# The first MoE's transposes, logits and block ends at a distance of four units instead of three

## The chip, the cores and the metric

The kernel runs on one core of a Trainium2 chip. The metric is the time of one execution on the device in microseconds (us), taken as the median of several runs. TensorE is called PE here (PEld is its weight load), VectorE DVE, ScalarE ACT, GpSimd POOL; SP only issues transfers.

## What is computed

Three layers in a row, all in float32: a clustered attention, a dense MoE with a rational activation, and a soft MoE. The change is in the middle one, with x the attention's output (1536 tokens by 512) and W_in 512 by 2048:

```
h = x @ w_in
P = a[0] + a[1]*h + a[2]*h**2 + a[3]*h**3
Q = 1.0 + abs(b[0])*abs(h) + abs(b[1])*h**2
g = P / (Q + 1e-6)
x2 = g @ w_out
logits = x2 @ phi                  # start of the soft MoE
d = softmax(logits over the tokens);  slot_input = d.T @ x2
c = softmax(logits over the slots);   out = c @ experts(slot_input)
```

The kernel never forms x2: it multiplies w_out by phi beforehand (`wphi`), so that the logits are g @ wphi, and it gathers d.T @ g before it multiplies by w_out.

## The kernel before

**The work.** The first MoE has three blocks of 512 tokens (`NB`), and each block sixteen units of 128 hidden columns (`NF`), so 48 units (`nunit`). A unit goes through five steps, each a small function:

- `h_mm(n)`: twelve matmuls on PE (lines L809, L810, L812) give the product h of unit n, 128 by 512, in one of three PSUM banks (`psH`). Two tiles of w_in (`w_load`, L652) have to be there.
- `s1(n)`: ACT makes u = |h| (L838) and the first linear term p (L839); POOL makes q from u (L840, L842); DVE goes on with p (L841, L843). L843 is the last to read h.
- `s2(n)`: ACT takes the reciprocal of q as exp(-ln q) into r, in one of two PSUM banks (L849, L850).
- `s3(n)`: DVE forms g with three operations (L857, L858, L859). L859 reads two SBUF tiles, q and p, and its result is g, held in the tile p.
- `s4(n)`: PE transposes g (four transposes, L870) into one of two PSUM banks, and ACT copies it to a buffer (L871). At every fourth unit PE also adds the logits of the last four units (eight matmuls, L876), and only then their four tiles p come free. At the sixteenth, DVE copies the logits out (L880).

After a block's sixteenth unit, `block_end` gives five steps, of which one is taken in each of the following turns: e0 (`lsum`, L892; DVE L893), e0b (transposes `lt`, L902, and ACT's exponentials, L905), e2 (transposes `dt`, L926), e3 (`dg`, 32 matmuls, L934, the gathering of g) and e1.

**The order.** The loop over n writes the order of PE and SP by hand: in turn n PE does `h_mm(n)`, then `s4(n - 3)`, then one step of a block end if there is one. PE's queue runs in this order, so whatever waits in `s4(n - 3)` holds `h_mm(n + 1)`. The order on ACT, DVE and POOL is made by the framework's planner, which plays the program through with costs of its own and takes instructions as they become ready there. On the chip each engine's queue runs strictly in that order. After the last product the loop runs three more turns, in which `warm(k)` puts 3, 4 and 1 matmuls on PE whose results nobody reads.

**After the loop** the last block end, the multiplication by w_out and the experts follow, fed by 1 MB weight loads (`wt`, L789) into buffers as these come free.

Of the kernel before, what the change touches and what calls it, by code (L numbers as in the profile page):

```python
# [8 lines left out]
F32 = mybir.dt.float32  # L9
# [53 lines left out]
def tile_kernel(ctx, tc, qT, kT, v, cenT, cenP, consts, constsb, ab, w_in, w_out, phi, w1, w2, out, dbg=None):  # L63
# [10 lines left out]
    NF = DFF // 128  # L74
# [574 lines left out]
    def w_load(n):  # L649
        for a in range(2):  # L650
            wsp[n, a] = w_p.tile([128, NCC, 128], F32R, tag="w", name="w")
            SP.dma_start(wsp[n, a].rearrange("p c n -> p (c n)").bitcast(F32),  # L652
                         w_in2[n % NF][:, a].rearrange("p c n -> p (c n)"))
# [38 lines left out]
    for n in range(-LEAD, NSL + 1):  # L692
        p, k = divmod(n, 12)
# [62 lines left out]
    g_p = bctx.enter_context(tc.tile_pool(name="gp", bufs=2, reuse_waits="tile"))  # L756
# [7 lines left out]
    def sl_tile(dt, name):  # L764
        return sl_p.tile([128, 4, 512], dt, tag="sl", name=name)
# [18 lines left out]
    def freed(alloc, n=1):  # L784
        for _ in range(n):
            if queue:
                key, src = queue.pop(0)
                t = alloc(F32, "wt").rearrange("p a b -> p (a b)")
                SP.dma_start(t, src)  # L789
                W[key] = (t, alloc)  # L790
# [8 lines left out]
    nunit = NB * NF  # L799
# [17 lines left out]
    def parts(n):  # L817

        return (slice(0, 256), slice(256, 512)) if n == nunit - 1 else (slice(0, 512),)

    def s1(n):

        h = hp.pop(n)
        u = g_p.tile([128, 512], F32, tag="u", name="u")
        q = g_p.tile([128, 512], F32, tag="q", name="q", bufs=4)
        p = g_p.tile([128, 512], F32, tag="g", name="p", bufs=7)
        sp[n] = dict(q=q, p=p)
        if n == nunit - 1:
            for w in parts(n):
                ACT.activation(u[:, w], h[:, w], AF.Abs)  # L830
                POOL.tensor_scalar(q[:, w], u[:, w], b_1, b_0, ALU.mult, ALU.add)
                POOL.tensor_tensor(q[:, w], q[:, w], u[:, w], ALU.mult)
            for w in parts(n):
                ACT.activation(p[:, w], h[:, w], AF.Identity, bias=a_n[2], scale=a_n[3])
                DVE.tensor_tensor(p[:, w], p[:, w], h[:, w], ALU.mult)
                DVE.scalar_tensor_tensor(p[:, w], p[:, w], a_n[1], h[:, w], ALU.add, ALU.mult)
            return
        ACT.activation(u, h, AF.Abs)  # L838
        ACT.activation(p, h, AF.Identity, bias=a_n[2], scale=a_n[3])  # L839
        POOL.tensor_scalar(q, u, b_1, b_0, ALU.mult, ALU.add)  # L840
        DVE.tensor_tensor(p, p, h, ALU.mult)  # L841
        POOL.tensor_tensor(q, q, u, ALU.mult)  # L842
        DVE.scalar_tensor_tensor(p, p, a_n[1], h, ALU.add, ALU.mult)  # L843
# [18 lines left out]
    def s4(n):  # L862
        t, f = divmod(n, NF)
        j, k = divmod(f, 4)
        g = gts[n]
        if k == 0:
            gsl[t, j] = sl_tile(F32, f"g{t}{j}")
        ps = psT.tile([128, 512], F32, tag="t", name="gt")
        for i in range(4):
            PE.transpose(ps[:, i * 128:(i + 1) * 128], g[:, i * 128:(i + 1) * 128], ident)  # L870
        ACT.copy(gsl[t, j][:, :, k * 128:(k + 1) * 128], ps.rearrange("p (i f) -> p i f", i=4))  # L871
        if k == 3:
            if j == 0:
                lps[t] = psL.tile([128, 512], F32, tag="l", name="l")
            for kk in range(4):
                PE.matmul(lps[t][32 * kk:32 * kk + 32, :], wphi[:, 4 * j + kk, :], gts.pop(n - 3 + kk),  # L876
                          start=(j == 0), stop=(j == 3))
            if j == 3:
                Ls[t] = keep.tile([128, 512], F32, tag="L", name="L")
                DVE.tensor_copy(Ls[t], lps.pop(t))  # L880


    def block_end(t):

        hold = {}
        nM, nM0 = mxs[:, t % 2:t % 2 + 1], mxs[:, 1 - t % 2:2 - t % 2]
        Sm, corr, sb = (mxs[:, i:i + 1] for i in range(2, 5))

        def e0():
            ps = psT.tile([128, 512], F32, tag="t", name="lsum")  # L890
            dT = hold["dT"] = Ls.pop(t)
            PE.matmul(ps, sum4, dT, start=True, stop=True)  # L892
            DVE.tensor_scalar(dT, ps, -1.0, None, ALU.mult, ALU.min, accum_out=nM)  # L893
            if t:
                DVE.tensor_tensor(nM, nM, nM0, ALU.min)

        def e0b():
            dT = hold["dT"]

            lt = psT.tile([128, 512], F32, tag="t", name="lt")  # L900
            for i in range(4):
                PE.transpose(lt[:, i * 128:(i + 1) * 128], dT[:, i * 128:(i + 1) * 128], ident)  # L902
            if t == NB - 1:
                hold["dT"] = a_tile("dT")
            ACT.activation(hold["dT"], dT, AF.Exp, scale=-1.0, bias=nM, accum_out=sb if t else Sm)  # L905
            if t:
                ACT.activation(corr, nM0, AF.Exp, scale=-1.0, bias=nM)
                DVE.scalar_tensor_tensor(Sm, Sm, corr, sb, ALU.mult, ALU.add)
            lv = lt.rearrange("p (i r s) -> p i r s", i=4, r=4)[:, :, 0, :]
            cm = keep.tile([128, 4], F32, tag="cm", name="cm")  # L910
            DVE.tensor_reduce(cm, lv, AX.X, ALU.min)
            DVE.tensor_tensor(ce[t], cm.unsqueeze(2).to_broadcast([128, 4, 32]), lv, ALU.subtract)

        def e1():
            cs = keep.tile([128, 4], F32, tag="cs", name="cs")
            c = ce[t]
            ACT.activation(c, c, AF.Exp)
            DVE.tensor_reduce(cs, c, AX.X, ALU.add)
            DVE.tensor_scalar(cs, cs, 1e-9, None, ALU.add)
            DVE.reciprocal(cs, cs)  # L920
            DVE.tensor_tensor(c, c, cs.unsqueeze(2).to_broadcast([128, 4, 32]), ALU.mult)

        def e2():
            ps = psT.tile([128, 512], F32, tag="t", name="dt")
            for i in range(4):
                PE.transpose(ps[:, i * 128:(i + 1) * 128], hold["dT"][:, i * 128:(i + 1) * 128], ident)  # L926
            d = hold["d"] = hold["dT"].rearrange("p (i s) -> p i s", i=4)
            ACT.copy(d, ps.rearrange("p (i s) -> p i s", i=4))

        def e3():  # L930
            ps = psT.tile([128, 512], F32, tag="t", name="dg")
            for i in range(4):
                for j in range(4):
                    PE.matmul(ps[32 * j:32 * j + 32, :], hold["d"][:, i, 32 * j:32 * j + 32], gsl[t, j][:, i, :],  # L934
                              start=(i == 0), stop=(i == 3))
            if t == 0:
                DVE.tensor_copy(U, ps)
            else:
                DVE.scalar_tensor_tensor(U, U, corr, ps, ALU.mult, ALU.add)
            if t == NB - 2:  # L940
                waiting.append(sl_tile)
            if t == NB - 1:
                freed(sl_tile, 4)

        return [e0, e0b, e2, e3, e1]

    def warm(k):

        for _ in range(k):
            ps = psH.tile([128, 512], F32, tag="h", name="warm")  # L950
            PE.matmul(ps[:, 0:256], ident, cst[:, 0:256], start=True, stop=True)

    ends = []


    manual = tc.manual_schedule(engines={mybir.EngineType.PE, mybir.EngineType.SP})
    manual.__enter__()
    for n in range(nunit + 3):
        if n + WAHEAD < nunit:
            w_load(n + WAHEAD)  # L960
        if waiting and n >= 3 and n % 3 == 0:
            freed(waiting.pop(0))
        if n < nunit:
            h_mm(n)
        if 0 <= n - 3:
            s4(n - 3)
            if (n - 3) % NF == NF - 1:
                ends += block_end((n - 3) // NF)
        if ends and (n - 3) % NF != NF - 1:
            ends.pop(0)()  # L970
        if n < nunit:
            s1(n)
        if 0 <= n - 1 < nunit:
            s2(n - 1)
        if n >= nunit:
            warm((3, 4, 1)[n - nunit])
        if 0 <= n - 2 < nunit:
            s3(n - 2)
    manual.__exit__(None, None, None)
# [12 lines left out]
    def a_tile(name, dt=F32):  # L992
        return a_p.tile([128, 512], dt, tag="a", name=name)
# [197 lines left out]
```

## Time and profile before

| what | value |
|---|---|
| median of 3 runs | 597.94 us (597.42 to 599.94) |
| the profiled execution, its own time | 601.37 us |
| its span, first to last instruction | 599.6 us |
| mean granted clock of TensorE | 0.989 of full |
| first MoE, first product to last transposes and logits | 337.3 to about 535 us |
| PE and DVE busy over the span | 557.7 us (93%) and 468.7 us (78%) |

The profiled execution is 3.43 us above the median; its span is 1.8 us shorter than its own time. Idle time is given in front of the instruction that ended it, with the instruction that released it. A matmul's duration reaches beyond the start of the next, as they are pipelined; the step from one start to the next tells the cost.

### The profile page before, as it was taken

How to read it: one execution, taken by the hardware profiler on the slowest of the kernel's cores; microseconds unless marked ns; L12 is line 12 of the kernel's file. 1: busy time of each engine (PE TensorE's matmuls, PEld its weight loads, DVE VectorE, ACT ScalarE, POOL GpSimd, SP SyncE). 2: the span in 40 equal slices, each digit the busy share in tenths (PEclk: the TensorE clock that was granted, in tenths of full speed). 3: DMA queues.
4: the chain of work that ended last, by engine and by line, in shares of the span. 5: the costliest groups of instructions: out<-in, count | busy, mean ns of one | idle time of the engine just before them, and what ended most of it. 6: DMA issues, size and time to landing. Idle time of an engine off the chain costs nothing.

```text
span 599.6 us, 9906 instructions
## 1 busy us (share of the span) xinstructions
PE 557.7 (93%) x3343; PEld 344.6 (57%) x3346; DVE 468.7 (78%) x817; ACT 393.2 (66%) x713; POOL 377.4 (63%) x487
## 2 busy tenths in 40 slices
PE   8899999999989999999899989999999999978995
PEld 3465555565555655555555667776667757753363
DVE  5779788798787987988984299999899998962033
ACT  3667777787677776787686487777578767740111
POOL 8749899697996988979658365565366545611000
PEclk9989999999999999999999999999999999989999
DMA  8613563354424633244343366766477547379996
GB/s 225 230 37 116 163 192 138 110 181 159 168 89 165 200 117 123 75 137 150 125 157 125 126 224 227 266 210 215 154 270 231 197 164 276 94 293 366 420 419 257
DMA packets 37906, 113.77 MB, mean 190 GB/s; under 512 B 5216, under 2 KB 5664, under 8 KB 33248
## 3 DMA queue, kind: packets, MB, share of 16 engines
q1 hardware_dynamic: 37856, 113.14, 54.1%
q8 instruction: 26, 0.43, 0.3%
q14 instruction: 24, 0.20, 0.1%
HBM read 96.02 MB, written 15.73 MB: 186 GB/s over the span
## 4 chain that ended last, share of the span: by engine, by line
PE 47%; DVE 26%; ACT 10%; POOL 8%; issue 7%; DMA 1%; SPq 0%; DVEq 0%; POOLq 0%; ACTq 0%
DVE neg L393 5%; PE s L383 5%; PE av L472 4%; PE s L458 4%; PE h L809 3%; PE h L812 3%; PE h L810 3%; PE s L384 3%; DVE p L859 3%; PE s L459 3%; PE pb L1042 3%; PE pb L1113 2%; DVE mh L564 2%; ACT neg L401 2%; DVE p L858 2%
## 5 line engine op out<-in xcount | busy, mean ns | idle before, releaser
L393 DVE TENSOR_SCALAR_CACHE_REDUCE neg<-s 128x768 f32<-128x768 f32 x96 | 91.3, 951 | 38.3 <-ACT neg L401 26.1
L463 ACT ACTIVATE e<-s 128x768 f32<-128x768 f32 x96 | 77.5, 807 | 58.3 <-PE s L459 58.2
L401 ACT ACTIVATE neg<-neg,nv 128x768 f32<-128x768 f32 x96 | 89.4, 932 | 9.2 <-DVE neg L393 8.9
L383 PE MATMUL s<-k,q 128*128 128x384 f32 x192 | 76.5, 398 | 13.3 <-DVE neg L393 9.5
L840 POOL TENSOR_SCALAR q<-u,babs 128x512 f32<-128x512 f32 x47 | 40.3, 858 | 75.9 <-ACT u L838 75.9
L472 PE MATMUL av<-e,vt 128*64 128x384 f32 x384 | 83.2, 512 | 0.2 <-ACT e L463 0.2
L809 PE MATMUL h<-xh,w 128*128 128x512 f32 x192 | 80.7, 420 | 0.0
L383 PEld LDWEIGHTS s<-k,q 128*128 128x128 f32 x192 | 36.6, 191 | 68.3 <-DVE neg L393 26.8
L810 PE MATMUL h<-xl,w 128*128 128x512 f32 x192 | 75.9, 395 | 0.0
L458 PE MATMUL s<-q,k 128*128 128x384 f32 x192 | 73.1, 381 | 0.7 <-DVE neg L393 0.5
L842 POOL TENSOR_TENSOR q<-q,u 128x512 f32<-128x512 f32 x47 | 63.8, 1357 | 3.9
L384 PE MATMUL s<-k,q 80*128 80x384 f32 x192 | 65.5, 341 | 0.0
L459 PE MATMUL s<-q,k 128*128 128x384 f32 x192 | 64.7, 337 | 0.0
L812 PE MATMUL h<-xh,w 128*128 128x512 f32 x192 | 52.7, 396 | 0.0
L579 POOL TENSOR_TENSOR w<-mh,ex 128x512 f32<-128x512 f32 x32 | 44.3, 1383 | 10.6 <-DMA w_out<-w 5.3
L859 DVE SCALAR_TENSOR_TENSOR p<-q,p 128x512 f32<-128x512 f32 (+1 forms) x49 | 49.2, 1005 | 0.1
L849 ACT ACTIVATE r<-q,epsc 128x512 f32<-128x512 f32 (+1 forms) x49 | 33.5, 684 | 21.9 <-POOL q L842 20.6
L838 ACT ACTIVATE u<-h 128x512 f32<-128x512 f32 x47 | 27.8, 591 | 27.7 <-PE h L812 27.7
L809 PEld LDWEIGHTS h<-xh,w 128*128 128x128 f32 x192 | 36.2, 189 | 16.9 <-issue 10.3
L458 PEld LDWEIGHTS s<-q,k 128*128 128x128 f32 x192 | 36.0, 188 | 16.2 <-issue 8.3
L841 DVE TENSOR_TENSOR p<-p,h 128x512 f32<-128x512 f32 x47 | 31.8, 677 | 16.9 <-ACT p L839 16.8
L812 PEld LDWEIGHTS h<-xh,w 128*128 128x128 f32 x192 | 36.3, 189 | 8.9
(193 smaller groups left out, 1219.3 us busy)
## 6 DMA issues: line engine op xcount, KB each, us to landing
wt<-w SPq DMA_DIRECT2D x32, 1024.0 KB, 8.0
w<-w_in SPq DMA_DIRECT2D x96, 256.0 KB, 3.1
raw<-w_in SPq DMA_DIRECT2D x16, 512.0 KB, 3.6
raw<-w_out SPq DMA_DIRECT2D x16, 512.0 KB, 3.4
w_in<-w SPq DMA_DIRECT2D x16, 512.0 KB, 2.7
rawk<-kT SPq DMA_DIRECT2D x14, 384.0 KB, 4.0
rawq<-qT SPq DMA_DIRECT2D x14, 384.0 KB, 3.6
w_out<-w SPq DMA_DIRECT2D x16, 256.0 KB, 3.3
```

The lines of the kernel that those rows point to most:

```text
L383: PE.matmul(ps[:, c, 0:HS], o["q1"][:, it], o["k1"][:, w], start=True, stop=False)
L384: PE.matmul(ps[:, c, 0:HS], o["q2"][0:80, it], o["k2"][0:80, w], start=False, stop=True)
L393: DVE.tensor_scalar(neg, s1s.pop((p, idx))[:, :, 0:HS], -1.0, None, ALU.mult, ALU.min, accum_out=nvs[p, half][0][:, 0, col:col + 1])
L401: ACT.activation(neg, neg, AF.Exp, scale=-1.0, bias=nv[:, 0, col:col + 1], accum_out=ssum[:, col:col + 1])
L458: PE.matmul(ps[:, h, 0:HS], o["k1"][:, jt], o["q1"][:, w], start=True, stop=False)
L459: PE.matmul(ps[:, h, 0:HS], o["k2"][:, jt], o["q2"][:, w], start=False, stop=True)
L463: ACT.activation(e, s2s.pop((p, k))[:, :, 0:HS], AF.Exp)
L472: PE.matmul(a[64 * h:64 * h + 64, 0:HS], vs[p][:, h, j, :], e[:, h, :], start=(j == 0), stop=(j == 5))
L809: PE.matmul(h, wh[:, c, :], xh[t][:, c, :], start=(c == 0), stop=False)
L810: PE.matmul(h, wh[:, c, :], xl[t][:, c, :], start=False, stop=False)
L812: PE.matmul(h, wl[:, c, :], xh[t][:, c, :], start=False, stop=(c == NCC - 1))
L859: DVE.scalar_tensor_tensor(p[:, w], q[:, w], 2.0, p[:, w], ALU.subtract, ALU.mult)
```

## The change

The distance becomes a constant, `LAG = 4`. Transposes, logits and block ends of unit n - 4 now follow the product of unit n on PE. There is one more turn at the end, with one more warming matmul in its place in the list, and the tiles p have eight buffers in place of seven, since each now lives one turn longer.

```
-        p = g_p.tile([128, 512], F32, tag="g", name="p", bufs=7)
+        p = g_p.tile([128, 512], F32, tag="g", name="p", bufs=8)
...
+    LAG = 4
...
-    for n in range(nunit + 3):
+    for n in range(nunit + LAG):
         if n + WAHEAD < nunit:
             w_load(n + WAHEAD)
         if waiting and n >= 3 and n % 3 == 0:
             freed(waiting.pop(0))
         if n < nunit:
             h_mm(n)
-        if 0 <= n - 3:
-            s4(n - 3)
-            if (n - 3) % NF == NF - 1:
-                ends += block_end((n - 3) // NF)
-        if ends and (n - 3) % NF != NF - 1:
+        if 0 <= n - LAG:
+            s4(n - LAG)
+            if (n - LAG) % NF == NF - 1:
+                ends += block_end((n - LAG) // NF)
+        if ends and (n - LAG) % NF != NF - 1:
             ends.pop(0)()
         if n < nunit:
             s1(n)
         if 0 <= n - 1 < nunit:
             s2(n - 1)
         if n >= nunit:
-            warm((3, 4, 1)[n - nunit])
+            warm((1, 3, 4, 1)[n - nunit])
         if 0 <= n - 2 < nunit:
             s3(n - 2)
```

## Rows read from the trace of the kernel before

**Rows 1.** The page's first part: busy time of each engine, its share of the span, its instructions.

```profile
PE 557.7 (93%) x3343; PEld 344.6 (57%) x3346; DVE 468.7 (78%) x817; ACT 393.2 (66%) x713; POOL 377.4 (63%) x487
```

**Rows 2.** The first MoE cut into six stretches (view of stretches, core 0). Columns: from:to in us, length, then busy us (and instructions) of PE, PEld, DVE, ACT, POOL, then the granted TensorE clock, DMA share and GB/s.

```profile
345.00:411.00 66.00, 62.90 (x312) 46.48 (x311) 64.24 (x91) 51.78 (x91) 39.05 (x36) 1.00 0.69 237
411.00:437.00 26.00, 24.96 (x145) 17.80 (x145) 23.42 (x38) 16.75 (x31) 12.80 (x12) 1.00 0.51 177
437.00:476.00 39.00, 37.62 (x189) 27.18 (x188) 38.19 (x53) 30.95 (x54) 22.78 (x22) 1.00 0.68 235
476.00:503.00 27.00, 25.89 (x149) 18.63 (x148) 24.31 (x42) 17.86 (x34) 13.02 (x13) 1.00 0.55 193
503.00:525.00 22.00, 21.31 (x110) 15.36 (x108) 21.39 (x31) 17.60 (x32) 13.38 (x12) 1.00 0.45 149
525.00:535.00 10.00, 7.44 (x38) 5.33 (x36) 7.41 (x15) 5.19 (x12) 2.92 (x4) 0.83 0.75 310
```

**Rows 3.** The groups by line inside 337 to 525 us, one of POOL's and the five DVE operations of a unit. Columns: line, engine, operation, tiles, shapes, count | busy us, mean ns | idle us before them and what ended it.

```profile
L859 DVE SCALAR_TENSOR_TENSOR p<-q,p 128x512 f32<-128x512 f32 x45 | 46.5, 1034 | 0.1
...
L840 POOL TENSOR_SCALAR q<-u,babs 128x512 f32<-128x512 f32 x47 | 40.3, 858 | 75.9 <-ACT u L838 75.9
...
L843 DVE SCALAR_TENSOR_TENSOR p<-p,ncoef,h 128x512 f32<-128x512 f32 x47 | 34.7, 737 | 0.4
...
L857 DVE SCALAR_TENSOR_TENSOR q<-q,epsc,r 128x512 f32<-128x512 f32 x46 | 33.9, 737 | 1.2 <-ACT r L850 1.1
...
L858 DVE SCALAR_TENSOR_TENSOR p<-p,ncoef,r 128x512 f32<-128x512 f32 x46 | 33.9, 736 | 0.0
...
L841 DVE TENSOR_TENSOR p<-p,h 128x512 f32<-128x512 f32 x47 | 31.8, 677 | 16.9 <-ACT p L839 16.8
```

**Rows 4.** The waits between 330 and 540 us: who waited for whom, us in total, times, longest us.

```profile
DVE p L841 <- ACT p L839: 16.8, 9, 8.8
...
PE gt L870 <- DVE p L859: 7.7, 13, 2.6
```

**Rows 5.** DVE in order of time, the instructions before which it sat idle. Columns: start us, duration us, engine, line, operation, tiles, count, [idle us before it <- what ended it].

```profile
341.70 0.69 DVE L841 TENSOR_TENSOR p<-p,h 128x512 f32<-128x512 f32 x1 [8.77 <-ACT p L839]
...
344.51 0.69 DVE L841 TENSOR_TENSOR p<-p,h 128x512 f32<-128x512 f32 x1 [1.34 <-ACT p L839]
...
370.11 0.69 DVE L841 TENSOR_TENSOR p<-p,h 128x512 f32<-128x512 f32 x1 [0.73 <-ACT p L839]
...
435.50 0.69 DVE L841 TENSOR_TENSOR p<-p,h 128x512 f32<-128x512 f32 x1 [2.45 <-ACT p L839]
...
496.78 0.69 DVE L841 TENSOR_TENSOR p<-p,h 128x512 f32<-128x512 f32 x1 [0.60 <-ACT p L839]
...
500.27 0.69 DVE L841 TENSOR_TENSOR p<-p,h 128x512 f32<-128x512 f32 x1 [2.02 <-ACT p L839]
```

**Rows 6.** PE in order of time around the first block end (same columns).

```profile
418.94 0.63 PE L926 MATMUL dt<-cst,L 128*128 128x128 f32 x4 [1.04 <-ACT p L839]
419.32 0.48 PE L809 MATMUL h<-xh,w 128*128 128x512 f32 x1
...
422.74 1.07 PE L876 MATMUL l<-p,wphi 128*32 128x512 f32 x8
423.62 3.62 PE L934 MATMUL dg<-g,L 128*32 128x512 f32 x32
427.17 0.50 PE L809 MATMUL h<-xh,w 128*128 128x512 f32 x1
...
430.44 0.48 PE L809 MATMUL h<-xh,w 128*128 128x512 f32 x1
```

**Rows 7.** DVE and then POOL in order of time at 511 to 515 us (same columns).

```profile
512.04 1.50 DVE L859 SCALAR_TENSOR_TENSOR p<-q,p 128x512 f32<-128x512 f32 x1
513.47 0.67 DVE L841 TENSOR_TENSOR p<-p,h 128x512 f32<-128x512 f32 x1
514.07 0.68 DVE L859 SCALAR_TENSOR_TENSOR p<-q,p 128x512 f32<-128x512 f32 x1
...
511.70 1.30 POOL L842 TENSOR_TENSOR q<-q,u 128x512 f32<-128x512 f32 x1
514.09 1.31 POOL L840 TENSOR_SCALAR q<-u,babs 128x512 f32<-128x512 f32 x1 [1.09 <-ACT u L838]
```

**Rows 8.** DVE and then PE in order of time near 400 us: the last read of product 15 (L843), the first matmul of product 18 (L809).

```profile
399.03 0.73 DVE L843 SCALAR_TENSOR_TENSOR p<-p,ncoef,h 128x512 f32<-128x512 f32 x1
...
401.67 0.48 PE L809 MATMUL h<-xh,w 128*128 128x512 f32 x1
```

**Rows 9.** The tail of the first MoE: the last half of DVE's last unit, PE's transposes of units 45 and 47, and three stretches of 2 us (columns as in rows 2).

```profile
532.53 0.42 DVE L859 SCALAR_TENSOR_TENSOR p<-q,p 128x256 f32<-128x256 f32 x1
...
527.80 0.63 PE L870 MATMUL gt<-cst,p 128*128 128x128 f32 x4 [2.56 <-DVE p L859]
...
533.41 0.60 PE L870 MATMUL gt<-cst,p 128*128 128x128 f32 x4
...
528.00:530.00 2.00, 2.00 (x9) 1.67 (x8) 1.52 (x3) 1.74 (x5) 0.24 (x1) 0.65 1.01 422
530.00:532.00 2.00, 2.00 (x8) 1.67 (x7) 1.98 (x6) 0.45 (x2) 0.00 (x0) 0.50 1.03 434
532.00:534.00 2.00, 2.00 (x15) 1.60 (x18) 0.91 (x2) 0.16 (x1) 0.00 (x0) 0.99 0.47 197
```

## The prediction

> **What bounds the kernel now.** I read the page first: PE is busy for 93% of the span and DVE for 78% [rows 1]. Those are means over three layers, so I cut the first MoE into stretches [rows 2]. There DVE is as full as PE: 64.24 of 66 us between 345 and 411, 38.19 of 39 between 437 and 476, 21.39 of 22 between 503 and 525. Only the two stretches that hold a block end differ: 23.42 of 26 and 24.31 of 27, so DVE is idle for 2.6 and 2.7 us there.
>
> The groups by line say why DVE is full [rows 3]. A unit's five operations have means of 1034, 737, 737, 736 and 677 ns. In order of time, one starts 0.07 us before the one ahead has ended in its record (513.47 against 512.04 + 1.50 [rows 7]), so a unit takes about 3.92 - 5 x 0.07 = 3.57 us of DVE. PE needs 430.44 - 427.17 = 3.27 us for a unit's product and transposes [rows 6], and each fourth unit 423.62 - 422.74 = 0.88 us more for logits: 3.27 + 0.22 = 3.49 us. The two engines are nearly balanced, and which one waits is a matter of how far one may run ahead of the other.
>
> The waits show both sides of that [rows 4]. PE waited 13 times for L859 before its transposes, 7.7 us in all, 2.56 of them in the tail [rows 9]. The reader should see what this is: PE is stopped by an engine that is full, not by one that is slow to answer. DVE waited 9 times for ACT's p, 16.8 us in all. Of these, 8.77 and 1.34 us are the start of the stage, where there is no product yet [rows 5]; that leaves 6.7 us. Most of the rest falls behind the block ends: 2.45 us at 435.50, 0.60 and 2.02 us at 496.78 and 500.27, and 0.73 us at 370.11.
>
> The cause stands in PE's order of time [rows 6]. Unit 22's product starts at 419.32 just behind `dt` (which had itself waited 1.04 us), and the next two products start at 427.17 and 430.44, because the logits and `dg` (427.17 - 422.74 = 4.43 us) lie between. A step of 7.85 us instead of 3.27 reaches DVE as missing input, once it has used up what PE had given ahead.
>
> **The change part by part.** It removes nothing and adds no computation apart from one warming step. It moves PE's `s4` and block ends behind one more product. I cost each part on the engine that sets the end, which is DVE up to its last L859 at 532.53 + 0.42 = 532.95 us [rows 9], and PE's chain behind it.
>
> *More work ahead of DVE at the block ends.* When PE turns to `dg`, one more product is done: DVE has up to one more unit, 3.57 us, to do. The holes to be covered are 2.45 and 2.62 us, each less than 3.57. That PE really has the lead follows from its waits: it was stopped by L859 of the unit three back, and the new order asks for the unit four back, which DVE has done about one unit's time earlier. Both holes go: -5.07 us. The bounds are 0 and -5.07. I take the full value, because 3.57 covers either with about 1 us to spare.
>
> *PE's waits for L859.* They go, at least in part, but I cost them at nothing: the work that hides them is DVE's own queue, full in these stretches, and a PE that arrives earlier meets the same L859s. What they return is the 0.73 us at 370.11, where DVE starved shortly after PE's first stalls: -0.73. The rest of the 6.7 us (6.7 - 5.07 - 0.73 = 0.9) I leave as a bound.
>
> *The start.* The first turn no longer asks for unit 0's transposes between products 3 and 4. DVE is already full then, and nothing changes: 0, with 0.73 us as the far bound by the nearest hole.
>
> *The tail.* One more unit's transposes, and unit 43's logits, now follow the last product. They are done while PE would wait for DVE; before, it stood idle 2.56 us for L859 of unit 45 [rows 9]. So 0. If that cover were gone, 0.60 us of transposes and 0.88 of logits would be added [rows 6, 9]. POOL is done earlier relative to DVE's last units, so that one or two L859s more run without it, each shorter by up to 1.03 - 0.68 = 0.35 us [rows 3, 7]: -0.3, bounds 0 and -0.7.
>
> *PE's clock in the tail.* Where PE sat idle and then did little, its granted clock fell to 0.65 in 528 to 530 and to 0.50 (1.2 GHz) in 530 to 532; behind the warming matmuls it is 0.99 from 532 on, just before the last transposes [rows 9]. After the change PE has little to do from an earlier point on, and the same groups of 3 and 4 warming matmuls precede the last transposes. Lower bound 0. Upper bound: the half clock lasts through the last logits and `dg`, whose time at full clock is 0.88 and 427.17 - 423.62 = 3.55 us [rows 6], and doubles it: +4.4 us. I take +0.1, since the same warming matmuls stand ahead.
>
> *Buffers and queues.* The eighth p buffer costs no time; with seven, each fourth unit's L839 would wait for the logits of four units back, now one turn later. SP's loads keep their order: the extra turn only takes one weight load that was queued right behind the loop. ACT's copy L871 and DVE's block-end pieces get new places from the planner, which no row of before shows. By the nearest row, the 0.73 us hole, once per block, this is up to 2.2 us either way; I take 0 and keep both.
>
> *Collisions of DVE and POOL.* L859 reads two SBUF tiles. At 512.04 it started while POOL's L842 ran (511.70 to 513.00), and took 1.50 us; at 514.07 it started just ahead of POOL's L840, took 0.68 us, and L840 took 1.31 against a mean of 0.858 [rows 3, 7]. The mean of 1034 ns is a mixture of both. The change shifts ACT and POOL against DVE. Bounds over 45 such L859s: 45 x (0.68 - 1.034) = -16 us and 45 x (1.50 - 1.034) = +21 us. Both ends need every instruction to meet alike. The mean is the nearest row to what an unknown shift would give, so I take 0, and +/-3 us (a mean between 0.97 and 1.10 us) for the range.
>
> The Trainium skill's page "SBUF — State Buffer", section "SBUF: two separate sides", says that a DVE operation with two SBUF inputs and a GpSimd operation that reads SBUF exclude each other, and that whichever starts first holds the shared ports for its whole length while the other blocks. The trace agrees at 512 and 514 us. The rule speaks against this change in that a saturated DVE meets POOL whenever POOL is fed sooner; by it, the outcome is the second rival below, while by the row's mean it is 0.
>
> **Sum.** -5.07 - 0.73 - 0.3 + 0.1 = -6.0 us. What follows the stage is a chain from the last L859, and the loads of the last layer hang on buffers that the same chain frees, so it moves as a whole. The profiled execution would go from 601.37 to 595.4 us, and its span from 599.6 to 593.6. It lies 3.43 us above the median shown, so the median becomes 597.94 - 6.0 = 591.9 us.
>
> **Rivals.**
>
> *Another cap takes the place.* Product n + 3 needs the bank of product n, which L843 frees. The tightest place that I found is 399.03 + 0.73 = 399.76 against product 18's start at 401.67, 1.9 us [rows 8]. If PE could gain only 1.9 us where it matters, the holes shrink to 0.55 and 0.72: still -3.8 - 0.2, about 594. If the planner also puts L843 or the block-end pieces later (+2.2 from above), the gain is about -1.8: 596 us, no measurable change. Against it: L843 of the units around the block end is done long before `dg`. 15 in 100 for a gain that is eaten in this way, 8 more for one that never arises because the holes only move to another place: 597 to 598 us.
>
> *Collisions get worse.* Place: L859 against L842. Each 0.1 us on the mean costs 4.5 us. From a mean of 1.034 + 6.0/45 = 1.17 us the gain is gone, and from 1.23 the kernel is slower by over 0.5% (3 us, about what a measurement here can tell from no change). If every other L859 met L842 as at 512.04 and the rest ran as now, the mean would be 1.27: +10.5 - 6.0 = +4.5, 602.4 us. For it: DVE's instructions repeat with a period of a few units, so a bad phase would repeat too. Against it: the mixture held over 45 units with different phases. 10 in 100.
>
> *PE's clock stays low* through the tail: +4.4 - 6.0, 596.3 us. The warming matmuls speak against it. 4 in 100, and 2 in 100 for it together with a cap, at no more than 599.
>
> *Collisions get better* by as much as 0.1 us: 587.4. 8 in 100.
>
> **How the numbers follow.** My forecast, 591.9, has 53 in 100, with its own range from 588.9 to 594.9 by the +/-3 of the collisions. Faster by over 0.5% (below 594.95): 53 + 8 and 3 of the 15 of the first rival, 0.64. Slower (above 600.9): 10, and 1 of the 2 for clock and cap together, 0.11. The rest, 0.25, is within 0.5%. The range leaves out the slower cases and a little below: 588.0 to 600.0.
>
> **What would show it.** Right: the holes before L841 behind the block ends shrink from 2.45 and 2.62 us to under 0.5 each; PE's waits for L859 inside the stage fall well below 7.7 us; the last L859 comes about 6 us earlier; its mean stays at 0.97 to 1.10 us; the last transposes run at full clock. Wrong: the holes stay, L859's mean passes 1.17 us, PE waits for L843 before L809, or the clock is 0.5 beyond the last transposes.

## The result: 1.5% less time, and no wait for L859 between the products

After the change the median is 589.37 us (588.53 to 590.35, 4 runs) against 598.94 for the kernel before in the same comparison (4 runs); the ratio is 0.9849, with a 95% interval of 0.9828 to 0.9870. That is 9.6 us less, where 6.0 were forecast. The profiled execution took 590.09 us (span 588.3) against 601.37 (599.6).

Where the 11.3 us of the two profiled executions went is seen from a few points in time. These are the first matmul of the first product and of the last, in PE's order of time, before and then after:

```profile
337.28 0.51 PE L809 MATMUL h<-xh,w 128*128 128x512 f32 x1
...
521.73 0.50 PE L809 MATMUL h<-xh,w 128*128 128x512 f32 x1
```

```profile
335.52 0.51 PE L809 MATMUL h<-xh,w 128*128 128x512 f32 x1
...
510.77 0.48 PE L809 MATMUL h<-xh,w 128*128 128x512 f32 x1
```

From the first of these to the last it was 521.73 - 337.28 = 184.45 us and is now 175.25: 9.20 us less ("the products" below). From the last product to DVE's copy of the last logits (L880, at 535.10 before and 523.89 after) it is 13.37 and 13.12 us. The stage began 1.76 us earlier, which lies in front of the changed code. 9.20 + 0.25 + 1.76 = 11.2 us, nearly all of it.

In the one execution of before that was profiled PE had less clock early on (20 to 40 us, before and then after; columns as in rows 2):

```profile
20.00:40.00 20.00, 18.19 (x99) 11.15 (x93) 15.20 (x33) 14.48 (x31) 10.79 (x17) 0.91 0.32 102
```

```profile
20.00:40.00 20.00, 18.15 (x110) 10.40 (x104) 16.48 (x35) 15.59 (x34) 10.97 (x18) 1.00 0.33 105
```

9% of 20 us is 1.8 us, so the clock may be the cause; it is not the only one, as a run at 1.00 there (the added DVE copy below) began the stage at 337.18. The kernel with the eighth buffer alone (first experiment below) has distance three too, and its profiled execution had 1.00 there. It began the stage at 335.40, its products took 184.46 us and the way to the logits' copy 12.78. Against it the change gains 9.21 us between the products and loses 0.34 behind them: 8.9 us, which is also what lies between the shortest executions of the two kernels, 597.42 and 588.53.

Waits of PE between the first product and the last, before (337 to 523 us) and then after (337 to 512). Columns as in rows 4:

```profile
PE gt L870 <- DVE p L859: 5.2, 12, 1.0
PE dt L926 <- ACT p L839: 2.2, 2, 1.1
```

```profile
PE dt L926 <- ACT p L839: 1.1, 1, 1.1
PE dt L926 <- DVE ce L912: 1.0, 1, 1.0
```

All twelve waits for L859 are gone from this stretch. Each cost more than the idle time in its row, as a matmul's record reaches beyond its work: the one at 383.36 us shows 0.34 us of idle time, and its step took 3.77 us where 3.23 do without a wait. Of the 9.20 us, 1.6 are unit 43's transposes and logits, which now follow the last product (a plain step is 3.26 us against 2.81 without transposes at the start; logits add 1.16). They are still done, but in the tail, where PE waits for DVE anyway. The other 7.6 are the waits.

The pace of four units far from a block end shows the waits too (first matmul of products 27 and 31 before, then of 28 and 32 after):

```profile
441.85 0.50 PE L809 MATMUL h<-xh,w 128*128 128x512 f32 x1
...
456.53 0.50 PE L809 MATMUL h<-xh,w 128*128 128x512 f32 x1
```

```profile
438.00 0.50 PE L809 MATMUL h<-xh,w 128*128 128x512 f32 x1
...
452.13 0.50 PE L809 MATMUL h<-xh,w 128*128 128x512 f32 x1
```

14.68 us before and 14.13 after. PE has no wait in the second stretch, so its own work is 14.13 / 4 = 3.53 us per unit; the prediction's 3.49 had the logits too short (0.88 us from the records, 1.16 from step to step). DVE's own work for four units was 4 x 3.57 = 14.28 us by the prediction's figure, a good part of it L859 blocked by POOL. So before the change four units took 0.55 us more than PE needed for them, and less than that above DVE's share.

But DVE's holes behind the block ends, which I had expected to fill, are all there (DVE in order of time, after; before: [rows 5]):

```profile
428.28 0.69 DVE L841 TENSOR_TENSOR p<-p,h 128x512 f32<-128x512 f32 x1 [0.30 <-ACT p L839]
...
431.93 0.69 DVE L841 TENSOR_TENSOR p<-p,h 128x512 f32<-128x512 f32 x1 [2.18 <-ACT p L839]
...
491.32 0.69 DVE L841 TENSOR_TENSOR p<-p,h 128x512 f32<-128x512 f32 x1 [0.61 <-ACT p L839]
...
494.81 0.69 DVE L841 TENSOR_TENSOR p<-p,h 128x512 f32<-128x512 f32 x1 [2.02 <-ACT p L839]
```

2.48 and 2.63 us, against 2.45 and 2.62. PE around the first block end shows why (after; before: [rows 6]):

```profile
415.64 0.63 PE L926 MATMUL dt<-cst,L 128*128 128x128 f32 x4 [0.96 <-DVE ce L912]
416.02 0.48 PE L809 MATMUL h<-xh,w 128*128 128x512 f32 x1
...
419.44 1.06 PE L876 MATMUL l<-p,wphi 128*32 128x512 f32 x8
420.32 3.62 PE L934 MATMUL dg<-g,L 128*32 128x512 f32 x32
423.87 0.50 PE L809 MATMUL h<-xh,w 128*128 128x512 f32 x1
...
427.13 0.48 PE L809 MATMUL h<-xh,w 128*128 128x512 f32 x1
```

From product to product across `dg` it is again 423.87 - 416.02 = 7.85 us, all of it work. DVE had no more in reserve than before. After, the last unit ahead of `dg` (23) had its L839 done at 420.78, and DVE came to its L841 at 423.26, 2.48 us later; before, it was unit 22, 423.68 and 426.81, 3.14 us. My reading is that DVE was no longer the slower of the two. It rests on the group of L859 (337 to 515 us) and the stretch that answers to the first of [rows 2]:

```profile
L859 DVE SCALAR_TENSOR_TENSOR p<-q,p 128x512 f32<-128x512 f32 x45 | 41.6, 926 | 0.1
```

```profile
345.00:411.00 66.00, 66.00 (x333) 50.50 (x332) 65.98 (x97) 54.80 (x95) 39.69 (x38) 1.00 0.69 245
516.00:518.00 2.00, 1.06 (x8) 0.80 (x7) 2.00 (x4) 1.95 (x6) 1.65 (x2) 1.00 1.07 451
518.00:520.00 2.00, 1.28 (x8) 0.83 (x7) 2.00 (x5) 1.65 (x5) 0.00 (x0) 1.00 0.99 418
520.00:522.00 2.00, 2.00 (x12) 1.65 (x11) 2.00 (x7) 0.59 (x1) 0.00 (x0) 1.00 0.94 397
```

L859's mean fell from 1034 to 926 ns, so a unit takes 3.57 - 0.11 = 3.46 us of DVE, just under PE's 3.53. Both engines now show 66 of 66 us busy in that stretch, so busy time doesn't tell which of them sets the pace; the added work in the last experiment does. The last three rows are the tail: the granted clock stays at 1.00 there, against 0.65 and 0.50 before [rows 9]. It need not be the change's doing. With the eighth buffer alone, at distance three, the same part of the tail has 1.00 as well:

```profile
526.00:528.00 2.00, 2.00 (x13) 1.79 (x14) 1.53 (x4) 1.74 (x5) 0.37 (x1) 1.00 0.98 410
528.00:530.00 2.00, 2.00 (x12) 1.63 (x11) 2.00 (x6) 0.74 (x2) 0.00 (x0) 1.00 1.05 442
```

### The profile page after: what moved, and what is told of

Same layout as the page of the kernel before. It is cut to its first block, busy times and chain, and to the rows that moved or that the text cites. A ratio compares the mean times of both kernels' runs of the same rounds, so it can differ in the third digit from the quotient of the medians.

```text
span 588.3 us, 9927 instructions
## 1 busy us (share of the span) xinstructions
PE 553.0 (94%) x3345; PEld 343.3 (58%) x3348; DVE 462.1 (79%) x817; ACT 392.4 (67%) x713; POOL 375.0 (64%) x487
## 4 chain that ended last, share of the span: by engine, by line
PE 56%; DVE 23%; ACT 8%; issue 6%; POOL 5%; DMA 2%; SPq 0%; DVEq 0%; POOLq 0%; ACTq 0%
PE h L809 6%; PE h L810 5%; PE h L812 5%; PE s L383 5%; DVE neg L393 5%; PE av L472 4%; PE s L458 4%; PE s L384 3%; PE s L459 3%; PE pb L1044 3%; PE pb L1115 3%; DVE mh L564 2%; ACT neg L401 2%; PE gt L870 2%; ACT e L463 2%
## 5 line engine op out<-in xcount | busy, mean ns | idle before, releaser
L840 POOL TENSOR_SCALAR q<-u,babs 128x512 f32<-128x512 f32 x47 | 39.6, 844 | 70.5 <-ACT u L838 70.5
L809 PE MATMUL h<-xh,w 128*128 128x512 f32 x192 | 80.6, 420 | 0.0
L842 POOL TENSOR_TENSOR q<-q,u 128x512 f32<-128x512 f32 x47 | 62.8, 1337 | 3.9
L809 PEld LDWEIGHTS h<-xh,w 128*128 128x128 f32 x192 | 36.2, 189 | 16.1 <-issue 1.9
L859 DVE SCALAR_TENSOR_TENSOR p<-q,p 128x512 f32<-128x512 f32 (+1 forms) x49 | 44.0, 901 | 0.1
L841 DVE TENSOR_TENSOR p<-p,h 128x512 f32<-128x512 f32 x47 | 31.8, 677 | 15.5 <-ACT p L839 15.4
```

Source lines behind the costliest of these rows:

```text
L809: PE.matmul(h, wh[:, c, :], xh[t][:, c, :], start=(c == 0), stop=False)
```

## The experiments

Two theories at first. C: the gain is DVE time that is no longer lost against POOL (L859's fall; 45 x 0.108 = 4.9 us), helped by the new order that the planner made for DVE. D: the gain is that PE no longer asks for a unit's transposes before the unit is through, and DVE's load matters little. Ratios are to the kernel before, run on the same chip.

**The eighth buffer alone.** `bufs=7` becomes `bufs=8` for p, at distance three.

> Distance three as before, but eight p buffers. Both theories: nothing, within 0.3% of before (about 598), as no p buffer was waited for. If the buffer were the cause, 590.

597.70 us, ratio 1.0007 (0.9986 to 1.0027): nothing. Its profiled execution began the stage at 335.40, like that of after, which confirms that the 1.76 us ahead of the stage are no part of the change.

**L859 without its second SBUF input,** at distances three and four:

```
-            DVE.scalar_tensor_tensor(q[:, w], q[:, w], epsc[:, 1:2], r[:, w], ALU.add, ALU.mult)
             DVE.scalar_tensor_tensor(p[:, w], p[:, w], a_n[0], r[:, w], ALU.add, ALU.mult)
-            DVE.scalar_tensor_tensor(p[:, w], q[:, w], 2.0, p[:, w], ALU.subtract, ALU.mult)
+            DVE.scalar_tensor_tensor(r[:, w], q[:, w], epsc[:, 1:2], r[:, w], ALU.add, ALU.mult)
+            DVE.scalar_tensor_tensor(p[:, w], r[:, w], 2.0, p[:, w], ALU.subtract, ALU.mult)
```

> Distance three; L859 reads its first operand from PSUM instead of SBUF (L857 writes its result over r), so that it has one SBUF input and should no longer meet POOL: its mean should fall from 1.03 to about 0.74 us, 13 us less of DVE over 45 units. Theory C (the gain of the change is DVE time that is no longer lost against POOL): most of the 9 us is gained here too, 588 to 592. Theory D (the gain is that PE no longer asks for a unit's transposes before the unit is through; DVE's load matters little): a unit gets through only 0.3 to 0.8 us sooner, so 2 to 4 us are gained, 594 to 596.

> The same freed L859 at distance four. Theory D (PE's own work sets the stage after the change): the same time as after, 588 to 590, less up to 1 us in the tail. Theory C: DVE still sets the stage, and 5 us or more are gained on after, 584 or less. The holes of DVE behind the block ends stay about 2 us by D.

At three: 587.47 us, ratio 0.9832 (0.9817 to 0.9847). At four: 586.22, ratio 0.9814 (0.9799 to 0.9830). The groups of L859 (337 to 520 us), at three and then at four:

```profile
L859 DVE SCALAR_TENSOR_TENSOR p<-r,p 128x512 f32<-128x512 f32 x47 | 32.0, 682 | 0.1
```

```profile
L859 DVE SCALAR_TENSOR_TENSOR p<-r,p 128x512 f32<-128x512 f32 x47 | 32.1, 682 | 0.1
```

At three this is what C expected, and D was wrong: with DVE freed, PE has no wait between 337 and 512 us at the old distance, and the products take 510.19 - 335.60 = 174.59 us. At four it is nearer to what D expected: 47 x 0.244 = 11.5 us less of DVE work than in after gain little more (172.72 us for the products, 2.53 less, most of them the two waits before `dt`, which are gone here too; 586.22 us lies below D's 587 and above C's 584). So neither theory holds alone. Either edit by itself ends PE's waits for L859; four units far from a block end take 14.13 us in both runs, as in after. The Trainium skill's page "SBUF — State Buffer", section "Who interferes with whom", says that a DVE instruction with at most one SBUF input, outside the modes with two ports, does not contend with GpSimd. The trace agrees: 682 ns on the mean, against 1034 with two.

The edit spares POOL as well: between 337 and 515 us the mean of L840 fell from 850 to 770 ns and that of L842 from 1354 to 1296. A quicker q could also have helped PE. But DVE stood only 1.2 us in all before L857 for r, which is made from q [rows 3], so little of PE's waiting can have come that way.

**Was it DVE's order?** To part the planner's order from the distance, I wrote the order of PE, ACT, DVE and POOL in the loop by hand, each taken from one of the two kernels. The controls:

> Control: the first MoE's loop with the order of PE, ACT, DVE and POOL all written out by hand, each engine as in before. Both theories: as before, 597 to 600.

> Control: all four engines in the order of after, by hand. Both theories: as after, 588 to 590.5.

598.30 us, ratio 0.9983 (0.9966 to 0.9999), and 589.70, ratio 0.9845 (0.9812 to 0.9877): each reproduces its model within 0.2%. Then DVE's list alone is exchanged (`ORDER_DVE`):

> PE and ACT in the order of before (distance three), only DVE in the order that the planner made for after. Theory C (the new DVE order meets POOL less): L859's mean falls to about 0.93 us and 4 to 5 us are gained, 593 to 595. Theory D (the distance on PE): 0 to 1.5 us, 597 to 599.

> PE and ACT in the order of after (distance four), only DVE in the order of before. Theory D: nearly all of the gain, 589 to 591, and PE without waits for L859. Theory C: half of it is lost, 593 to 595, and L859's mean is 1.03 us again.

With after's DVE order at distance three: 623.02 us, ratio 1.0401 (1.0365 to 1.0437). Nobody expected that. PE's waits between 337 and 545 us:

```profile
PE gt L1058 <- DVE p L1046: 8.0, 12, 1.3
PE lt L1096 <- DVE L L1088: 7.3, 2, 3.7
PE dt L1136 <- ACT g L1063: 3.8, 2, 1.9
```

That order puts the block-end pieces and L859 (here L1046) where they suit a PE that asks a turn later: besides the 12 waits for L859, PE now waits 7.3 us before `lt` for DVE's piece of the block end. L859's mean was 976 ns. This order is no gain without its distance.

With before's DVE order at distance four: 595.93 us, ratio 0.9943 (0.9922 to 0.9964), which fits neither theory as written. The products took 513.59 - 336.20 = 177.39 us, so 7.1 of the 9.2 us were gained, as D has it. The tail then loses more: 16.49 us from the last product to the logits' copy, against 13.12 in after. The rows are PE's waits for an h bank (337 to 535 us), DVE in order of time before the copies of the block logits and in the tail, and L859's group (337 to 520 us):

```profile
PE h L809 <- DVE p L1014: 3.1, 5, 0.8
```

```profile
405.22 0.69 DVE L1076 COPY L<-l 128x512 f32<-128x512 f32 x1 [2.50 <-PE l L1071]
...
468.57 0.69 DVE L1076 COPY L<-l 128x512 f32<-128x512 f32 x1 [1.99 <-PE l L1071]
...
525.23 0.48 DVE L1036 SCALAR_TENSOR_TENSOR q<-q,epsc,r 128x256 f32<-128x256 f32 x1 [2.43 <-ACT r L1031]
```

```profile
L1046 DVE SCALAR_TENSOR_TENSOR p<-q,p 128x512 f32<-128x512 f32 x45 | 42.1, 936 | 0.1
```

L859's mean is 936 ns in the old order, so its fall doesn't come from the new order. L1014, the reader of h (L843 before), is what PE waits for: the first rival of the prediction, in small. This order puts the copy of a block's logits (L1076) where they are ready at distance three; at four PE delivers them a turn later, and DVE stands 2.50 and 1.99 us for them. Four of PE's five waits for h (at 409.78, 414.48, 473.39 and 478.18) follow within 10 us.

**The freed L859 in exactly the old order** (hand-written order of before, L857 and L858 of a unit exchanged), since the planner had made a new order for the freed kernel too:

> Distance three, all four engines by hand in the order of before, with the freed L859 (L857 and L858 of a unit change places, as L857 now writes over r). Theory C2 (at three, the time that DVE loses against POOL is what makes PE wait): PE's waits for L859 vanish as in the freed run with the planner's own order, 587 to 590. If that run was fast because the planner gave it another DVE order: 595 to 598, and PE still waits for L859 ten times or more.

590.74 us, ratio 0.9869 (0.9826 to 0.9911), a little above the 587 to 590 expected. PE waited for L859 once (1.2 us) in place of twelve times, and the products took 176.09 us. At distance three, time lost by DVE against POOL was what made PE wait; the order was not.

**PE's two last waits.** The first two block ends return `[e0, e0b, e1, e2, e3]` instead of `[e0, e0b, e2, e3, e1]`, at distance four.

> Distance four, and in the first two block ends the step without PE work comes before dt, so that dt and dg come one turn later. After the change the only waits of PE inside the stage are 0.96 and 1.11 us before dt. Theory D: these two go and the time falls by about 2 us from after, to 587. Theory C (DVE sets the stage): nothing, 589.

588.18 us, ratio 0.9836 (0.9821 to 0.9851); the interval overlaps that of after, so the median does not settle it. The trace does: both waits are gone, and the products took 509.54 - 335.84 = 173.70 us, 1.55 less. The most telling rows are DVE's (L859's group, 337 to 520 us, and the two holes at the block ends):

```profile
L859 DVE SCALAR_TENSOR_TENSOR p<-q,p 128x512 f32<-128x512 f32 x47 | 46.6, 993 | 0.1
```

```profile
437.42 0.69 DVE L841 TENSOR_TENSOR p<-p,h 128x512 f32<-128x512 f32 x1 [0.18 <-ACT p L839]
...
497.12 0.69 DVE L841 TENSOR_TENSOR p<-p,h 128x512 f32<-128x512 f32 x1 [1.71 <-ACT p L839]
```

Here L859 lost more against POOL than in after (993 ns, not 926), and the products were still faster: the holes shrank instead, from 2.48 to 0.18 and from 2.63 to 1.71 us. That is 47 x 0.067 = 3.1 us more on L859 and 3.2 us less in holes: on this DVE, which doesn't set the pace, the one took the place of the other. As `dt` and `dg` moved too, the run doesn't show which of them led.

**Who sets the stage?** Theory F: at four PE's own work; at three PE waits and has slack. Theory G: DVE in both. One matmul whose result is overwritten is added to each product:

```
         h = psH.tile([128, 512], F32, tag="h", name="h")
+        PE.matmul(h, wh[:, 0, :], xh[t][:, 0, :], start=True, stop=True)
```

> Distance three with one more matmul of 512 columns per product on PE (its result is overwritten): 48 x 0.23 = 11.2 us of PE work. Theory F (at three PE waits because a unit is not through; its own work has slack of about 7 us there): most of it goes into the waits, +2 to +5 us on before, 600 to 603. If PE's own work set the time in before: +11, 609. Theory G (DVE sets the time in both kernels): +0 to +4 as well.

> The same added matmuls at distance four. Theory F (PE has no wait left there and its own work sets the stage): the whole 11 us is seen, 600 to 601, and DVE's holes grow. Theory G: DVE sets the stage and hides half of it or more, 595 or less.

And one small DVE copy per unit, at four, just ahead of L843:

```
+        DVE.tensor_copy(scr, h[:, 0:16])
         DVE.scalar_tensor_tensor(p, p, a_n[1], h, ALU.add, ALU.mult)
```

> Distance four with one more small DVE copy (16 columns, some 0.1 us) per unit: 47 x 0.1 = 4 to 5 us of DVE work. Theory F: DVE's holes (5.9 us behind the start) take most of it, 589 to 591. Theory G: all of it is seen, 593 to 595.

PE's 11 us cost 0.6% at three (601.58 us, ratio 1.0059, 1.0037 to 1.0082), that is 3.5 us, and at four they took the ratio from 0.9849 to 1.0014 (0.9992 to 1.0037; 599.44 us), that is 9.9 us. F holds: the slack that PE had at three is gone at four. The traces say so from the other side. At three the products took 187.68 us, 3.23 more than before where some 11 were added, and of PE's waits for L859 the rows show one of 0.4 us: 7.8 us went into these waits and the two before `dt`, which are gone. At four they took 184.35 us, 9.10 more; the rest went into the two waits before `dt`, gone here too. DVE's holes behind the first block end grew from 2.48 to 4.04 us, as F expected, and at three they are 4.02, against 2.45 before: they are long where PE is the slower engine (at three and then at four):

```profile
433.27 0.69 DVE L842 TENSOR_TENSOR p<-p,h 128x512 f32<-128x512 f32 x1 [2.00 <-ACT p L840]
...
436.76 0.69 DVE L842 TENSOR_TENSOR p<-p,h 128x512 f32<-128x512 f32 x1 [2.02 <-ACT p L840]
```

```profile
434.73 0.69 DVE L842 TENSOR_TENSOR p<-p,h 128x512 f32<-128x512 f32 x1 [2.02 <-ACT p L840]
...
438.22 0.69 DVE L842 TENSOR_TENSOR p<-p,h 128x512 f32<-128x512 f32 x1 [2.02 <-ACT p L840]
```

The DVE copy gave 591.34 us, ratio 0.9881 (0.9857 to 0.9905), up to 2 us more than after, with intervals that overlap. F's direction holds, but not its way. The copy took 162 ns by its record, and the holes did not shrink; L859 (L862 here) lost less against POOL instead (337 to 525 us). What the run lost lies in PE's two waits before `dt`, 3.3 us against 2.1 in after:

```profile
L845 DVE COPY scr<-h 128x16 f32<-128x16 f32 x47 | 7.6, 162 | 0.0
```

```profile
L862 DVE SCALAR_TENSOR_TENSOR p<-q,p 128x512 f32<-128x512 f32 x47 | 41.3, 879 | 0.1
```

```profile
PE dt L929 <- ACT g L874: 1.8, 1, 1.8
PE dt L929 <- DVE ce L915: 1.5, 1, 1.5
```

## Why the prediction was right, and where its reasons were wrong

- **Direction and range:** right. Forecast 591.9 (588.0 to 600.0), measured 589.37. The own range of the likeliest case, 588.9 to 594.9, held it too. But its mechanism was wrong, and that the number fits is luck, as the last point shows.
- **"PE's waits for L859 ... I cost them at nothing: the work that hides them is DVE's own queue":** this step failed, and it is the gain. I read a full DVE as the bound. But a part of its busy time was L859 blocked by POOL, so DVE's 3.57 us per unit was no fixed cost, and four units took 14.68 us where PE's own work is 14.13. With PE free of these waits it became 3.46. The waits were worth 7.6 us, not 0.73.
- **"Both holes go: -5.07 us":** measured 0. The hole behind a block end is PE's extra work as seen from DVE (7.85 us between two products, the same after). My reading is that a lead that covers it builds up only while DVE is the slower engine. It fits the runs: with more work on PE the holes behind the first block end are 4.02 and 4.04 us, and where DVE lost more against POOL (`dt` one turn later) they shrank to 0.18 and 1.71.
- **Collisions, taken as unchanged (0.97 to 1.10):** the mean went to 0.926, below that range. I had listed this as the case of "collisions get better by as much as 0.1 us" with 8 in 100. The second rival, collisions that make it slower, did not come.
- **The tail at 0, and -0.3 for L859s without POOL:** the extra transposes and logits are hidden there, as I wrote (at a clock of 1.00 it is 12.78 us with the eighth buffer alone and 13.12 after from the last product to the logits' copy), and the -0.3 did not come. But as PE set the pace, work moved from between the products into the tail is a gain, and the sum has no term for it: 1.6 us for unit 43. With L859 freed the two distances show it nearly alone: 174.59 + 12.66 = 187.25 us at three and 172.72 + 13.03 = 185.75 at four.
- **The clock at +0.1:** no cost came; it was 1.00 in the three stretches shown. The 0.65 and 0.50 of before, on which the term rests, are not tied to distance three: with the eighth buffer alone, at three, it was 1.00 there, and with before's DVE order at distance four 0.83 between 520 and 530 us.
- **The h banks as a new cap:** no wait in after; five short ones (3.1 us) with before's DVE order.
- So the sum came near by errors of opposite sign: 5.1 us put on holes that stayed, 6.9 too little on waits that went, and 1.6 left out for unit 43.

## What to carry to other kernels

When two engines of a pipeline wait for each other in turn, add up the work of each without its waits for the other, and without what a third engine makes it lose; the change gains the waits of the engine that has the larger sum. An engine that is busy all the time is the bound only if its instructions last as long when it is left alone: compare one instruction's mean with its shortest record. An order made for one distance lost time at the other here, both ways.

## What the runs showed that I had not expected

DVE's busy time is elastic: the same L859 had means of 1034, 993, 936, 926 and 879 ns in kernels that differ in the order or in small additions, and 682 once one of its SBUF inputs was moved to PSUM. Why the mean is highest in before, where PE restarts on L859's end, is only argued (each restart would then bring POOL's next multiply at the same place). One run bears on it: with the added matmuls at distance three PE hardly waits for L859 any more, and the mean (337 to 525 us, L860 there) is 927 ns without any change of the distance:

```profile
L860 DVE SCALAR_TENSOR_TENSOR p<-q,p 128x512 f32<-128x512 f32 x44 | 40.8, 927 | 0.2
```

So the fall needs no change of the distance. In these runs it goes with the end of the waits; why is left open. Freeing L859 at distance four has the lowest median of the study, 586.22 us, though its interval (0.9799 to 0.9830) overlaps that of the freed kernel at three and of `dt` one turn later.
